# E and F stacked on 128 partitions and turned together, the last unit of the first chunk normalised by VectorE, A's turns placed anew

## Chip, cores and metric

One core of one Trainium2 chip. The metric is the device time of one execution in microseconds; the median of several executions is given. The kernel before takes 569.17 us (569.0 to 570.17 in 4 runs).

Below, "weights" without more are those of the feed-forward part. "Projection" is the product of E with K; the program's name for its result is `kvp`.

## The reference, cut to what matters

```python
k_proj = einsum('ks,bhsd->bhkd', E, k)           # E, F: 64 x 1024; k, v: 8 x 8 x 1024 x 64, f32
v_proj = einsum('ks,bhsd->bhkd', F, v)
attn   = softmax(q @ k_proj.T / 8)               # per head, 64 keys
x      = (attn @ v_proj) as 8192 x 512
out    = (silu(x @ w_gate) * (x @ w_val)) @ w_out   # 512 -> 1536 -> 512
```

## The kernel before

The work is a stream of 16 chunks of 512 tokens. Attention of later chunks is woven into the feed-forward matmuls of earlier ones, so TensorE hardly ever stands still. Only the first chunk has nothing to hide behind: its K, E, F, V, q and weights have to arrive, E and F have to be turned (their 1024 positions must lie on partitions), and then come the projection of K, the scores, the softmax in four "units", the turn of the attention matrix A, the product with V, and the first feed-forward matmuls. The change touches this start only.

```python
def warm(n):                       # n matmuls on zeros; keep TensorE's clock up
    ps = bank("v", [P, CW], FP32, "warm")
    for _ in range(n): nc.tensor.matmul(out=ps[:], lhsT=zeros[:, 0:P], rhs=zeros[:], ...)

def u_N(b, u, eng=nc.gpsimd):      # normalise one unit: ee * rr, 128 x 512
    ...
    eng.tensor_tensor(out=..., in0=ee..., in1=rr...to_broadcast([P, 4, 2, KP]), op=ALU.mult)

# transfers at the start
for i in range(2):
    nc.scalar.dma_start(out=kraw[i][:], in_=k[0, 2*i : 2*i+2]...)      # heads 0-1, 2-3
for which, src in (("E", E), ("F", F)):
    raw = const.tile([KP, S], FP32, name=f"{which}raw")                # 64 partitions each
    (nc.sync if which == "E" else nc.scalar).dma_start(out=raw[:], in_=src)
...
# order of work, cut and shortened (u_T turns q, u_KT0 turns the projected K, u_S scores and exp,
# u_A turns A, u_V0 projects V, u_PV1 and u_PV2 multiply A with V, f_mm feed-forward matmuls)
warm(11); turn(E); warm(4)
cast kraw -> kb (VectorE; half of head 3 by ScalarE)
u_KV(0, "k", (0, 4)); warm(1)      # first projection
u_T, u_KT0; turn(F, half 0); u_T; u_S(0, 0) ...; turn(F, half 1); warm(1)
u_KV(0, "k", (4, 8)) ...           # second projection, then scores, units 2, 1, 3
u_N(0, 3)                          # on GpSimd
u_V0(0, 2); u_PV2; warm(1); u_V0(2, 3); u_A(0, 2); u_V0(3, 4)
u_PV1(2); u_PV1(3); u_A(0, 1)
f_mm(gate of f=0); u_A(0, 3); u_PV2; f_mm(value of f=0) ...
```

The casting loads (K's heads 4 to 7, q, V, the weights) are issued by GpSimd on one queue; E, F and K's heads 0 to 3 come by the hardware queues of SyncE and ScalarE.

The softmax here doesn't subtract the row's maximum and nothing guards it: scores larger than these inputs give would overflow.

Of the kernel before, what the change touches and what calls it, by code (L numbers as in the profile page):

```python
# [12 lines left out]
BF16 = mybir.dt.bfloat16  # L13
FP32 = mybir.dt.float32
# [3 lines left out]
S = 1024  # L18
D = 64
KP = 64  # L20
DM = H * D
DFF = 1536
P = 128
NJ = S // P
# [10 lines left out]
def kernel(  # L35
# [19 lines left out]
    nc = tc.nc  # L55
    scale = 1.0 / float(D) ** 0.5

    const = ctx.enter_context(tc.tile_pool(name="const", bufs=1))
# [15 lines left out]
    BD = [const.tile([P, H, P], BF16, name=f"BD{i}") for i in range(2)]  # L74
    BDV = [const.tile([P, NPAIR, P], BF16, name=f"BDV{i}") for i in range(2)]
    ks = [const.tile([P, H, D], BF16, name=f"ks{i}") for i in range(2)]
    ET = const.tile([P, NJ, KP], BF16, name="ET")
    FT = const.tile([P, NJ, KP], BF16, name="FT")

    wg = w_pool.tile([P, NKT, DFF], BF16, name="wg")  # L80
    wv = w_pool.tile([P, NKT, DFF], BF16, name="wv")
# [51 lines left out]
    def bank(where, shape, dt, name):  # L133
        pool, tag = banks[where]
        return pool.tile(shape, dt, name=name, tag=tag)

    def copy(eng, out, in_):
        (nc.scalar.copy if eng is nc.scalar else eng.tensor_copy)(out=out, in_=in_)  # L138
# [152 lines left out]
    def u_N(b, u, eng=nc.gpsimd):  # L291
        ch, w = divmod(u, 4)
        g, i = divmod(w, 2)
        if (b, ch) in BY_DMA:
            if (b, ch, "d") not in AA:
                AA[b, ch, "d"] = aw.tile([P, 4, H, KP], BF16, name="AAd", tag="AAd")
            a = AA[b, ch, "d"][:, 2 * i : 2 * i + 2, 4 * g : 4 * g + 4, :]
        else:
            a = AA[b, u] = aw.tile([P, 2, 4, KP], BF16, name="AA", tag="AA", bufs=4)
            a = a[:]  # L300
        eng.tensor_tensor(  # L301
            out=a.rearrange("p j h k -> p h j k"),
            in0=ee.pop((b, u))[:],
            in1=rr.pop((b, u))[:].unsqueeze(3).to_broadcast([P, 4, 2, KP]),
            op=ALU.mult,
        )
# [45 lines left out]
    def u_PV1(b, ch, pr, i, eng):  # L352

        ps = ps_a.tile([P, CW // 2], FP32, name="pv", tag="pa")
        nc.tensor.matmul(
            out=ps[:].rearrange("p (j t) -> p j t", t=P),
            lhsT=BDV[b % 2][:, pr, :],
            rhs=AT[b, ch][:, 2 * i : 2 * i + 2, pr, :],
            start=True,
            stop=True,  # L360
        )
        copy(eng, xT[b, ch][:, pr, 256 * i : 256 * (i + 1)], ps[:])
# [4 lines left out]
    half = {}  # L367
# [110 lines left out]
    with tc.manual_schedule():  # L478

        kb[0] = kv_pool.tile([P, H, NJ, D], BF16, name="kb", tag="kb")  # L480
        kraw = [aw.tile([P, 2, NJ * D], FP32, name="kraw", tag=tag) for tag in ("qTd", "AAd")]
        for i in range(2):
            nc.scalar.dma_start(
                out=kraw[i][:],
                in_=k[0, 2 * i : 2 * i + 2].rearrange("h (p j) d -> p h (j d)", j=NJ),
            )
        ef = []
        for which, src in (("E", E), ("F", F)):
            raw = const.tile([KP, S], FP32, name=f"{which}raw")
            (nc.sync if which == "E" else nc.scalar).dma_start(out=raw[:], in_=src)  # L490
            ef.append(raw)
        load_q(0, 0, (0, 2))
        load_k(0, 4, 8)
        zeros = const.tile([P, CW], BF16, name="zeros")
        nc.vector.memset(zeros[:], 0.0)
        make_identity(nc, ident_fp[:])
        make_identity(nc, ident_bf[:])
        nc.vector.memset(ks[0][64:P], 0.0)

        def turn(which, at, halves=(0, 1)):  # L500
            for half in halves:
                ps = bank(at, [P, 4, KP], FP32, "efp")
                for i in range(4):
                    j = 4 * half + i
                    nc.tensor.transpose(  # L505
                        out=ps[:, i, :],
                        in_=ef[which][:, bass.ds(j, P, step=NJ)],
                        identity=ident_fp[:KP, :KP],
                    )
                js = slice(4 * half, 4 * half + 4)  # L510
                copy(nc.scalar, (ET, FT)[which][:, js, :], ps[:])

        def warm(n):

            ps = bank("v", [P, CW], FP32, "warm")
            for _ in range(n):
                nc.tensor.matmul(  # L517
                    out=ps[:], lhsT=zeros[:, 0:P], rhs=zeros[:],
                    start=True, stop=True,
                )  # L520


        dve, act = nc.vector, nc.scalar
        load_q(0, 0, (2, 4))
        load_v(0, (0, 4, 6, 8))
        load_w_gv(0, 1)
        load_w_gv(1, 2, (0,))
        warm(11)
        turn(0, "v")
        warm(4)  # L530
        for h in range(4):
            for n in range(2):
                eng = act if (h, n) == (3, 1) else dve
                ds = slice(256 * n, 256 * (n + 1)) if h == 3 else slice(0, 512)
                if n == 0 or h == 3:
                    copy(eng, kb[0][:, h].rearrange("p j d -> p (j d)")[:, ds], kraw[h // 2][:, h % 2, ds])
        nc.vector.memset(BD[0][:], 0.0)
        u_KV(0, "k", (0, 4), at="y")
        warm(1)
        u_T(0, 0, "a", act)  # L540
        u_KT0((0, 2), "vg", (dve, dve, dve, act))
        turn(1, "a", (0,))
        u_T(0, 2, "a", act)
        u_S(0, 0, "g")
        u_R(0, 0)
        u_N(0, 0)
        load_w_gv(1, 2, (1,))
        load_w_gv(2, 4, (0,))
        turn(1, "a", (1,))
        warm(1)  # L550
        u_KV(0, "k", (4, 8), at="y")
        warm(1)
        u_KT0((2, 4), "vg", (dve, dve, act, act))
        u_T(0, 1, "a", dve)
        u_T(0, 3, "a", dve)
        u_S(0, 2, "g")
        u_A(0, 0, dve)
        u_R(0, 2)
        u_N(0, 2)
        u_S(0, 1, "g")  # L560
        u_R(0, 1)
        u_N(0, 1)
        u_S(0, 3, "v")
        u_R(0, 3)
        u_N(0, 3)
        u_V0(0, 2, "y")
        u_PV2(0, 0, 0, 0, act)
        warm(1)
        u_V0(2, 3, "y")
        u_A(0, 2, act)  # L570
        u_V0(3, 4, "v")
        u_PV1(0, 0, 2, 0, dve)
        u_PV1(0, 0, 3, 0, act)
        u_A(0, 1, dve)
        load_w_gv(2, 4, (1,))
        f_mm(0, 0, 0, 0)
        u_A(0, 3, act)
        u_PV2(0, 0, 0, 1, dve)
        f_mm(0, 0, 1, 0)
        f_mm(0, 1, 0, 0)  # L580
        u_PV2(0, 0, 1, 1, act)
        f_mm(0, 1, 1, 0)
        nc.vector.memset(ks[1][64:P], 0.0)
        nc.vector.memset(BD[1][:], 0.0)
        nc.vector.memset(BDV[1][:], 0.0)
        load_w_gv(4, 6)
        load_q(0, 1, hs=(0, 4))
        load_w_gv(6, 8)
        load_q(0, 1, hs=(4, 8))
        load_w_gv(8, 10)  # L590
        load_w_gv(10, 12)
        load_q(1, 0)
        load_k(1)
        load_wo(0)
        load_wo(1)

        for i, u in enumerate(range(4, 8)):
            put(11 + i, u_T, 0, u)
            put(13 + i, u_S, 0, u)
            put(14 + i, u_R, 0, u)  # L600
            put(14 + i, u_N, 0, u)
            put((17, 18, 20, 21)[i], u_A, 0, u, nc.scalar)
        put(19, u_PV, 0, 1, 0)
        put(20, u_PV, 0, 1, 1)
        put(22, u_PV, 0, 1, 2)
        put(22, u_PV, 0, 1, 3, nc.vector)
        put(20, load_v, 1)
        put(20, load_q, 1, 1)
        for b in range(1, B):
            place(b)  # L610
        for b in range(2, B):
            s0 = 48 * (b - 1) - (20 if b == 3 else 24)
            at = (43, 43, 44, 45) if b == 2 else (s0, s0 + 2, s0 + 4, s0 + 6)
            put(at[0], load_k, b)
            put(at[1], load_v, b)
            put(at[2], load_q, b, 0)
            put(at[3], load_q, b, 1)

        for s in slots:
            slots[s].sort(key=lambda x: x[0] not in (load_k, load_v, load_q))  # L620


        ypart = defaultdict(list)
        for c in range(B * CH - 1):
            for n in range(NFT):
                f = n if c else 4 + (2 * n + 1) // 3
                ypart[(c + 1) * NFT + f].append((c, n))

        for t in range(NIT):
            c, f = divmod(t, NFT)  # L630
            i = 1 if t < 2 else None
            f_g(c, f, i)
            run_slot(2 * t)
            f_v(c, f, i)
            for a in ypart.pop(t, ()):
                f_y(*a)
            run_slot(2 * t + 1)
        for n in range(9):
            f_y(B * CH - 1, n)
        f_y_last(B * CH - 1, 3)  # L640
        assert not slots and not ypart
# [29 lines left out]
```

## Time and profile before

| what, in the trace of before | us |
|---|---|
| span | 567.5 |
| TensorE busy | 561.1 |
| first projection starts | 8.24 |
| second projection starts | 12.47 |
| first value matmuls start (`vps`, f = 0) | 21.21 |
| value matmuls of f = 6 start | 33.43 |

The four starts are the milestones of this document. A shift of the last one is a shift of the end, because from there on TensorE works without a wait.

### The profile page before, as it was taken

The page shows a single profiled execution, that of the slowest core. Times are in us where ns is not written, and L with a number is a line of the kernel's source. Part 1 is how long each engine was busy: PE and PEld are TensorE (multiplying, and loading weights), DVE is VectorE, ACT ScalarE, POOL GpSimd, SP SyncE. Part 2 cuts the span into 40 slices and gives each one's busy share as a digit, 9 for nine tenths or more (in the row PEclk, how much of TensorE's full clock was granted, in tenths as well). Part 3 has the DMA queues.
Part 4 walks back from the last instruction along what each step waited for, and adds up shares of the span by engine and source line. Part 5 has one row for each costly group of instructions (what it writes and reads, how often), then busy time and mean ns, then how long its engine had stood idle before and what let it go on. Part 6 is the DMA issues. An engine that isn't in the chain of part 4 may idle for free.

```text
span 567.5 us, 7942 instructions
## 1 busy us (share of the span) xinstructions
PE 561.1 (99%) x2970; PEld 266.5 (47%) x2970; DVE 338.9 (60%) x576; ACT 235.7 (42%) x416; POOL 111.0 (20%) x124
## 2 busy tenths in 40 slices
PE   8999999999999999999999999999999999999997
PEld 4654444444444444444444444444444444444444
DVE  3786664766476645766466655666547665545550
ACT  3564452444435443443434434354343543443322
POOL 6951250124012400123002230023100220000000
PEclk9999999999999999999999999999999999999999
DMA  9999999729913795029940499106990213101012
GB/s 207 184 199 190 168 146 199 138 57 185 194 49 74 116 198 114 38 57 166 182 80 37 76 185 203 38 19 112 192 180 19 61 39 69 38 37 38 19 38 93
DMA packets 111159, 62.91 MB, mean 111 GB/s; under 512 B 64272, under 2 KB 102416, under 8 KB 111120
## 3 DMA queue, kind: packets, MB, share of 16 engines
q0 software_dynamic: 42816, 29.36, 36.1%
q1 hardware_dynamic: 67392, 31.46, 26.6%
q10 hardware_dynamic: 912, 1.57, 1.0%
q8 instruction: 23, 0.38, 0.3%
q14 instruction: 16, 0.13, 0.1%
HBM read 60.29 MB, written 16.78 MB: 136 GB/s over the span
## 4 chain that ended last, share of the span: by engine, by line
PE 95%; DMA 2%; POOL 1%; DVE 1%; ACT 0%; issue 0%; POOLq 0%
PE yps L415 29%; PE vps L377 28%; PE gps L377 28%; PE kvp L150 3%; PE sc L271 2%; PE pv L328 2%; DMA wv<-in_moe_w_val_dram 2%; PE warm L517 1%; PE efp L505 0%; POOL AA L301 0%; POOL wv L118 0%; POOL wg L118 0%; DVE BD L138 0%; PE kTp L194 0%; PE qTp L237 0%
## 5 line engine op out<-in xcount | busy, mean ns | idle before, releaser
L396 DVE SCALAR_TENSOR_TENSOR s<-th,gps 128x512 f32<-128x512 f32 x192 | 130.4, 679 | 134.6 <-ACT th L389 134.1
L377 PE MATMUL vps<-xT,wv 128*128 128x512 bf16 (+1 forms) x776 | 197.5, 377 | 0.4 <-DMA wv<-in_moe_w_val_dram 0.3
L377 PE MATMUL gps<-xT,wg 128*128 128x512 bf16 (+1 forms) x776 | 197.7, 377 | 0.1
L415 PE MATMUL yps<-wo,hT 128*128 128x512 bf16 (+1 forms) x780 | 194.5, 376 | 0.0
L389 ACT ACTIVATE th<-gps 128x512 f32<-128x512 f32 x192 | 114.6, 597 | 159.0 <-PE gps L377 153.9
L401 DVE TENSOR_TENSOR hT<-s,vps 128x512 bf16<-128x512 f32 x192 | 132.0, 687 | 20.4 <-DVE s L396 0.5
L301 POOL TENSOR_TENSOR AAd<-ee,rr 128x512 bf16<-128x512 f32 x56 | 58.3, 1043 | 342.3 <-issue 184.8
L415 PEld LDWEIGHTS <-hT 128*128 128x128 bf16 x780 | 76.2, 98 | 89.9
L377 PEld LDWEIGHTS <-wv 128*128 128x128 bf16 x776 | 73.8, 98 | 84.2 <-issue 2.9
L377 PEld LDWEIGHTS <-wg 128*128 128x128 bf16 x776 | 74.0, 98 | 81.3 <-issue 1.2
L425 ACT ACTIVATE ysb<-yps 128x512 f32<-128x512 f32 (+1 forms) x65 | 38.4, 591 | 77.7 <-PE yps L415 77.7
L138 ACT CAST xT<-pv 128x512 bf16<-128x512 f32 (+1 forms) x62 | 35.9, 582 | 52.3 <-PE pv L328 50.3
L286 DVE TENSOR_REDUCE zz<-ee 128x8 f32<-128x512 f32 x64 | 43.5, 679 | 22.4 <-ACT ee L275 22.4
L275 ACT ACTIVATE ee<-sc 128x512 f32<-128x512 f32 x64 | 37.9, 595 | 19.7 <-PE sc L271 18.5
L271 PEld LDWEIGHTS <-qTd 128*128 128x128 bf16 x224 | 17.2, 98 | 13.2 <-DMA qTd<-qb 0.2
L328 PE MATMUL pv<-AT,BDV 128*128 128x512 bf16 x60 | 22.4, 379 | 0.1
L271 PE MATMUL sc<-BD,qTd 128*128 128x128 bf16 x224 | 21.6, 219 | 0.0
L288 DVE RECIPROCAL rr<-zz 128x8 f32<-128x8 f32 x64 | 13.0, 203 | 6.7 <-DVE zz L286 0.5
L108 POOL DMA_DIRECT2D qb<-in_q_dram x18 | 16.3, 908 | 1.4 <-POOLq L655 0.8
L150 PE MATMUL kvp<-kb,ET 128*64 128x512 bf16 (+1 forms) x72 | 15.5, 358 | 0.0
L162 DVE CAST BDV<-kvp 64x256 bf16<-64x256 f32 x7 | 3.0, 426 | 20.0 <-ACT ks L158 17.8
L150 PE MATMUL kvp<-vb,FT 128*64 128x512 bf16 x56 | 13.4, 382 | 0.0
(64 smaller groups left out, 137.7 us busy)
## 6 DMA issues: line engine op xcount, KB each, us to landing
out_dram<-ysb SPq DMA_DIRECT2D x63, 256.0 KB, 2.3
qb<-in_q_dram POOLq DMA_DIRECT2D x14, 512.0 KB, 18.0
kb<-in_k_dram POOLq DMA_DIRECT2D x7, 1024.0 KB, 11.0
vb<-in_v_dram POOLq DMA_DIRECT2D x7, 1024.0 KB, 14.4
wo<-in_moe_w_out_dram POOLq DMA_DIRECT2D x2, 768.0 KB, 21.8
wg<-in_moe_w_gate_dram POOLq DMA_DIRECT2D x5, 256.0 KB, 8.0
wv<-in_moe_w_val_dram POOLq DMA_DIRECT2D x5, 256.0 KB, 9.6
kraw<-in_k_dram ACTq DMA_DIRECT2D x2, 512.0 KB, 4.9
```

The lines of the kernel that those rows point to most:

```text
L138: (nc.scalar.copy if eng is nc.scalar else eng.tensor_copy)(out=out, in_=in_)
L150: nc.tensor.matmul(out=t[lo : lo + 64, h0:h1].rearrange("p h d -> p (h d)"), lhsT=w[:, j, :], rhs=src[b][:, h0:h1, j, :], start=(j == 0), ...
L271: nc.tensor.matmul(out=ps[:, n, :], lhsT=t[:, n, :], rhs=BD[b % 2][:, 4 * g + n, :], start=True, stop=True)
L275: nc.scalar.activation(out=e[:].rearrange("p h j k -> p (h j k)"), in_=ps[:].rearrange("p a k -> p (a k)"), func=AF.Exp, scale=scale,)
L286: nc.vector.reduce_sum(out=z[:], in_=e[:], axis=AX.X)
L301: eng.tensor_tensor(out=a.rearrange("p j h k -> p h j k"), in0=ee.pop((b, u))[:], in1=rr.pop((b, u))[:].unsqueeze(3).to_broadcast([P, 4, 2 ...
L377: nc.tensor.matmul(out=ps[:, ts], lhsT=(wg, wv)[w][:, kt, f * P : (f + 1) * P], rhs=x[:, kt, ts], start=(kt == 0), stop=(kt == NKT - 1),)
L389: nc.scalar.activation(out=th[:], in_=ps[:], func=AF.Tanh, scale=0.5)
L396: nc.vector.scalar_tensor_tensor(out=s1[:], in0=th[:], scalar=1.0, in1=g[:], op0=ALU.add, op1=ALU.mult)
L401: nc.vector.tensor_tensor(out=hT[c][:, f, :], in0=s1[:], in1=ps[:], op=ALU.mult)
L415: nc.tensor.matmul(out=yy[c][:, cs], lhsT=hT[c][:, f, i * P : (i + 1) * P], rhs=wo[:, f, cs], start=(f == 0), stop=(f == NFT - 1),)
L425: nc.scalar.activation(out=ysb[:, cs], in_=yy[c][:, cs], func=AF.Copy, scale=0.5)
```

## The change

It means to have E and F in one tile of 128 partitions, so that eight turns do the work of sixteen and no turn of F interrupts the middle; to give the third normalisation in a row to VectorE, so that GpSimd is free to issue weights; and to turn A before the first gate matmuls.

```diff
-    ET = const.tile([P, NJ, KP], BF16, name="ET")
-    FT = const.tile([P, NJ, KP], BF16, name="FT")
+    EF = const.tile([P, NJ, 2 * KP], BF16, name="EF")
+    ET, FT = EF[:, :, 0:KP], EF[:, :, KP : 2 * KP]
...
-        for which, src in (("E", E), ("F", F)):
-            raw = const.tile([KP, S], FP32, name=f"{which}raw")
-            (nc.sync if which == "E" else nc.scalar).dma_start(out=raw[:], in_=src)
+        efraw = const.tile([P, S], FP32, name="efraw")
+        for i, src in enumerate((E, F)):
+            nc.sync.dma_start(out=efraw[64 * i : 64 * i + 64], in_=src)
...
-        warm(11)
-        turn(0, "v")
-        warm(4)
+        warm(12)
+        turn_ef()          # 8 transposes of 128 x 128 f32, 2 copies of 128 x 512 by ScalarE
+        warm(2)
...  (head 3 cast by VectorE alone; the two turns of F and three warm matmuls around
...   the second projection's work go, warm(3) comes)
-        u_N(0, 3)
+        u_N(0, 3, dve)
...
-        warm(1)
         u_V0(2, 3, "y"); u_A(0, 2, act); u_V0(3, 4, "v"); u_PV1(0, 0, 2, 0, dve)
+        u_A(0, 1, dve)
         u_PV1(0, 0, 3, 0, act)
-        u_A(0, 1, dve)
+        u_A(0, 3, act)
         load_w_gv(2, 4, (1,))
         f_mm(0, 0, 0, 0)
-        u_A(0, 3, act)
```

More of the change, by code (lines that the diff above doesn't have):

```diff
@@ L486 @@
             )
-        ef = []
-        for which, src in (("E", E), ("F", F)):
-            raw = const.tile([KP, S], FP32, name=f"{which}raw")
-            (nc.sync if which == "E" else nc.scalar).dma_start(out=raw[:], in_=src)
-            ef.append(raw)
+        efraw = const.tile([P, S], FP32, name="efraw")
+        for i, src in enumerate((E, F)):
+            nc.sync.dma_start(out=efraw[64 * i : 64 * i + 64], in_=src)
         load_q(0, 0, (0, 2))
@@ L498, with turn_ef @@
         nc.vector.memset(ks[0][64:P], 0.0)
-        def turn(which, at, halves=(0, 1)):
-            for half in halves:
-                ps = bank(at, [P, 4, KP], FP32, "efp")
+        def turn_ef():
+            for half in range(2):
+                ps = bank("gv"[half], [P, 4, 2 * KP], FP32, "efp")
                 for i in range(4):
-                    j = 4 * half + i
                     nc.tensor.transpose(
                         out=ps[:, i, :],
-                        in_=ef[which][:, bass.ds(j, P, step=NJ)],
-                        identity=ident_fp[:KP, :KP],
-                    )
-                js = slice(4 * half, 4 * half + 4)
-                copy(nc.scalar, (ET, FT)[which][:, js, :], ps[:])
+                        in_=efraw[:, bass.ds(4 * half + i, P, step=NJ)],
+                        identity=ident_fp[:],
+                    )
+                nc.scalar.copy(out=EF[:, 4 * half : 4 * half + 4, :], in_=ps[:])
         def warm(n):
@@ L527 @@
         load_w_gv(1, 2, (0,))
-        warm(11)
-        turn(0, "v")
-        warm(4)
+        warm(12)
+        turn_ef()
+        warm(2)
         for h in range(4):
-            for n in range(2):
-                eng = act if (h, n) == (3, 1) else dve
-                ds = slice(256 * n, 256 * (n + 1)) if h == 3 else slice(0, 512)
-                if n == 0 or h == 3:
-                    copy(eng, kb[0][:, h].rearrange("p j d -> p (j d)")[:, ds], kraw[h // 2][:, h % 2, ds])
+            copy(dve, kb[0][:, h].rearrange("p j d -> p (j d)"), kraw[h // 2][:, h % 2])
         nc.vector.memset(BD[0][:], 0.0)
         u_KV(0, "k", (0, 4), at="y")
-        warm(1)
         u_T(0, 0, "a", act)
         u_KT0((0, 2), "vg", (dve, dve, dve, act))
-        turn(1, "a", (0,))
         u_T(0, 2, "a", act)
@@ L548 @@
         load_w_gv(2, 4, (0,))
-        turn(1, "a", (1,))
-        warm(1)
+        warm(3)
         u_KV(0, "k", (4, 8), at="y")
@@ L564 @@
         u_R(0, 3)
-        u_N(0, 3)
+        u_N(0, 3, dve)
         u_V0(0, 2, "y")
         u_PV2(0, 0, 0, 0, act)
-        warm(1)
         u_V0(2, 3, "y")
```

## The prediction

> **What bounds the kernel now.** I read the page first, then the waits of TensorE, then the timeline and the chain of waits of the first 40 us, then the landing times of the transfers that the change touches.
>
> ```profile
> PE 561.1 (99%) x2970; PEld 266.5 (47%) x2970; DVE 338.9 (60%) x576; ACT 235.7 (42%) x416; POOL 111.0 (20%) x124
> PEclk9999999999999999999999999999999999999999
> ...
> PE 95%; DMA 2%; POOL 1%; DVE 1%; ACT 0%; issue 0%; POOLq 0%
> ```
>
> TensorE (PE) is busy for 561.1 of 567.5 us at full clock. What is not useful matmul work lies in the start-up, before the steady stream at about 24 us. The diff touches nothing else: the order of instructions of the changed program differs from the old one only there. Only some 20 us of 569 can react, and much of that is fixed by transfers. The waits of TensorE in the first 60 us:
>
> ```profile
> PE warm L517 <- DVE zeros L495: 1.2, 1, 1.2
> PE pv L343 <- ACT BDV L185: 0.5, 1, 0.5
> PE vps L377 <- DMA wv<-in_moe_w_val_dram: 0.3, 1, 0.3
> PE pv L355 <- ACT AT L138: 0.2, 1, 0.2
> ```
>
> The third line is a wall: the first matmul of the value branch cannot start before its weights land. The timeline puts it here:
>
> ```profile
> 7.99 0.77 POOL L118 DMA_DIRECT2D wv<-in_moe_w_val_dram  x1
> ...
> 21.21 0.61 PE L377 MATMUL vps<-xT,wv 128*128 128x256 bf16 x4 [0.30 <-DMA wv<-in_moe_w_val_dram]
> ```
>
> Issued at 7.99 and 13.2 us under way (the longest landing in the view of that line), it lands at 21.17. The GpSimd queue moves about 200 GB/s from 8 us on without a hole, so this landing is set by the bytes queued ahead. A second wall is in the chain of waits:
>
> ```profile
> 19.02 1.03 POOL AA L301
> 20.05 0.76 POOL wv L118
> ...
> 23.74 9.64 DMA wv<-in_moe_w_val_dram
> ```
>
> These weights land at 33.38 and their first matmul starts at 33.43. The matmul group before it started at 32.93 and streams 0.22 us (the chain gives 0.22 for such groups of four), so TensorE stood about 0.28 us there: an estimate from these numbers. Time won before 21 us is kept only if both landings come earlier too. The part that is moved, E's and F's way to the first projection, is this:
>
> ```profile
> 0.74 0.58 SPq L490 DMA_DIRECT2D Eraw<-in_E_dram  x1
> 1.77 0.54 ACTq L490 DMA_DIRECT2D Fraw<-in_F_dram  x1
> 6.15 1.11 PE L505 MATMUL efp<-ident_fp,Eraw 64*128 64x64 f32 x8
> 7.27 0.86 DVE L138 CAST kb<-kraw 128x512 bf16<-128x512 f32 x2 [1.70 <-DMA kraw<-in_k_dram]
> 8.24 1.06 PE L150 MATMUL kvp<-kb,ET 128*64 128x256 bf16 x8
> ```
>
> E lands at 6.02 (5.3 us after issue), the second K transfer at 7.25 (6.0 us), F at 8.92 (7.2 us). The 11 warming matmuls end just when E arrives. Today the first projection at 8.24 waits for E and for K's casts but not for F: F is turned in two halves between later work, at 10.01 and 11.57.
>
> **What the Trainium skill says.** Page "DMA: Bandwidth & Descriptors", section "Queues, rings and completion order": each DMA engine takes turns between the queues at the granularity of a packet. The trace agrees: the packet records show the first K transfer at 1.88 to 3.9 us, E (64 packets of 4096 bytes on SyncE's queue) at 3.6 to 4.7, the second K transfer at 4.3 to 6.6, F at 6.7 to 7.7; on one engine after another E's first packet starts about 5 ns after K's last, and K's second 5 ns after E's. So the queues alternated, one whole transfer's share at a time. The same page, "Issuing engines are not separate DMA queues": moving an issue to another engine saves only issue time, since all run on the same 16 DMA engines. Page "TensorE: Matmul & The Clock Gate", section "The HAM clock gate": the clock drops only after an idle window of some 3.4 us. No such gap is in this trace, and a wait of 2 us should not cool it. Page "SBUF — State Buffer", section "SBUF: two separate sides": a VectorE operation with two SBUF inputs and a GpSimd operation that reads SBUF lock each other out. No row here shows that pair, so it is open.
>
> **The change part by part.**
>
> 1. E and F by one queue. F's issue moves from 1.77 (third on ScalarE) to about 1.32 (0.74 + 0.58, second on SyncE), a saving of 0.45 us at issue. If queues alternate as above, the order stays K, E, K, F. F then follows the second K transfer directly, without the 0.4 us hole that the packets show between the end of most of its packets (6.28) and F's first (6.69). I expect F to land at about 8.2 to 8.6 instead of 8.92.
>
> 2. Turning together. Eight transposes over 128 columns replace sixteen over 64. Eight of 64 take 1.11 us, with starts some 0.12 us apart (6.2 to 7.0 in the view of that tile). Twice the columns means about 0.23 us apart: 8 x 0.23 = 1.8 us, an estimate. The two F halves disappear from the middle (0.60 + 0.58 us in the chain), so 1.11 + 1.18 = 2.29 becomes 1.8: 0.5 us less TensorE work. ScalarE has two copies of 0.59 us (row of 128x512 f32 to bf16) for four of 0.37 to 0.39: 0.3 us less. But all 1.8 us now lies ahead of the first projection, and so does F's landing. This is the cost that I think decides.
>
> 3. Start of the projection. Landing 8.4 + 0.1 + 1.8 + two warm matmuls of 0.22 = 10.5 us, against 8.24: 2.2 us later. TensorE idles from the end of the 12 warm matmuls (1.19 + 12 x 0.43 = 6.4; a cold one takes 0.43) to 8.4.
>
> 4. What the middle gives back. From the start of the first projection to the start of the second is 4.23 us now (8.24 to 12.47). The way to the first scores is unchanged, because the BD copies set it (10.06 to 11.27). After the scores, at 11.64, F's half and one warm matmul go (0.58 + 0.32) and three warm matmuls come (0.65): 0.2 us back. The warm matmul between the small projections of V goes too: 0.2 us.
>
> 5. K's casts. Head 3 is no longer split with ScalarE; a whole head takes 0.477 us against 0.517 for the half beside ScalarE. No cost.
>
> 6. The last unit normalised by VectorE. On GpSimd one takes 1.04 us and the third runs from 19.02 to 20.05; on VectorE such a two-tensor operation takes 0.69 us (row of hT), in a hole of VectorE from 18.43 to 19.60. GpSimd issues the next weights 1.03 us earlier. But the queue is full at that time, so I count at most the 0.28 us at the second wall.
>
> 7. The A turns. Their four-matmul groups (0.22 us each) move ahead of the first gate matmuls. The work is the same and the order only helps if their inputs are ready: 0.
>
> Sum at the first wall: +2.2 - 0.2 - 0.2 = +1.8 us for the work arriving there. TensorE has 0.30 us of waiting to spend at 21.21, leaving +1.5. The second wall absorbs another 0.28: +1.2, or 570.4 us.
>
> **The rivals.** (a) F follows E directly on its queue, before the second K transfer. The 12 warm matmuls (end 6.4) look sized for such a landing near 6.6. K then lands about 0.8 us later, at 8.1, its two casts end at 9.1, and the projection starts at 9.1 (+0.9). Parts 4 and the 0.30 us of slack swallow nearly all of it, and part 6 gives up to 0.28: 569.0 us. For it speaks the sizing; against it the alternation of packets. (b) GpSimd's earlier issues bring the later weights down and a denser start of the hardware queues (the dip at 4.5 to 5.5 us, about 200 GB/s between stretches of 340) brings everything queued behind 0.3 to 0.5 us earlier. Both walls then move and TensorE keeps up: 568.5. Against it: the latency of 9.64 us at 23.74 is queueing, not issue. (c) The shared port holds VectorE's normalisation until GpSimd's runs out at 19.05. Then VectorE's xT copy, now 19.60, is 0.15 us later or so, which the wall hides under (a) and adds under the main path: 570.6. (d) TensorE cools while it waits for F; matmuls of 0.43 instead of 0.22 us for one window would add 1 us or more: 571.5.
>
> **Range and chances.** I weigh the main path with (c) and (d) at a little over half (570.4 and up) and (a) with (b) at a little under half (568.5 to 569.1). The middle is 569.8 us. The three runs of before already spread from 569.0 to 570.17, so a range of 568.5 to 571.2 should hold it 8 times in 10. Two per cent is 11.4 us, most of the start-up, which nothing here can move: within 2% at 0.98, faster 0.01, slower 0.01.
>
> **What would show it.** The landing of F (issue plus time under way): near 8.4 means the main path, near 6.6 rival (a). The start of the first kvp group: 10.5 or 9.1. The first transposes of efp: 8 in about 1.8 to 2 us. A TensorE wait before efp of about 2 us, or none. The vps group now at 21.21: at about 22.7 and without a DMA wait on the main path, still near 21.2 and with one under (a), below 20.9 under (b). GpSimd should show three AA groups in the first 24 us instead of four, and the weight issue now at 20.00 near 19.1 plus the delay of the work before. I am wrong if the second wall moves by a microsecond with GpSimd's issues, if the transposes are much longer than 0.23 us apart, or if something beyond 40 us changes at all.

## The result, and the profile after

The changed kernel takes 570.6 us (570.07 to 571.49 in 4 runs) against 569.17. The ratio is 1.0023, with a 95% interval of 1.0005 to 1.0041. (Ratios here are the mean time of one kernel's fast runs over that of the other's fast runs of the same rounds, so not quite the ratio of the medians.) The loss is clear of noise and far within 2%.

First the line of engine busy times and the clock, from the page of the changed kernel; they answer to the lines of before in the prediction:

```profile
PE 560.7 (99%) x2961; PEld 266.3 (47%) x2961; DVE 340.4 (60%) x577; ACT 235.1 (41%) x413; POOL 110.1 (19%) x123
PEclk8999999999999999999999999999999999999999
```

TensorE has 0.4 us less to do, and the span is 1.6 us longer (569.1). So the time went into waits, and the first digit of the clock row is an 8 where it was a 9. The waits of TensorE in the first 60 us of the changed kernel (total, times, longest):

```profile
PE efp L503 <- DMA efraw<-in_F_dram: 1.9, 1, 1.9
PE warm L514 <- DVE zeros L493: 1.2, 1, 1.2
PE pv L343 <- ACT BDV L185: 0.5, 1, 0.5
PE sc L271 <- DVE BD L138: 0.5, 1, 0.5
PE pv L355 <- ACT AT L138: 0.2, 1, 0.2
PE aTp L317 <- DVE xT L138: 0.2, 1, 0.2
```

A wait of 1.9 us for F has come in, and the wait for the value weights has gone. The timeline of the same stretch (start, duration, engine, line, operation):

```profile
1.19 5.30 PE L514 MATMUL warm<-zeros 128*128 128x512 bf16 x12 [1.19 <-DVE zeros L493]
1.38 0.57 SPq L489 DMA_DIRECT2D efraw<-in_F_dram  x1
8.41 1.12 PE L503 MATMUL efp<-ident_fp,efraw 128*128 128x128 f32 x8 [1.92 <-DMA efraw<-in_F_dram]
9.89 1.91 PE L150 MATMUL kvp<-kb,EF 128*64 128x256 bf16 x8
14.74 1.06 PE L150 MATMUL kvp<-kb,EF 128*64 128x256 bf16 x8
20.74 1.13 DVE L301 TENSOR_TENSOR AA<-ee,rr 128x512 bf16<-128x512 f32 x1
23.13 0.60 PE L377 MATMUL vps<-xT,wv 128*128 128x256 bf16 x4
35.06 1.03 PE L377 MATMUL vps<-xT,wv 128*128 128x512 bf16 x4
```

Read it by the milestones. The first projection starts 1.65 us later (9.89 against 8.24), the second 2.27 later, the value matmuls 1.92 later, those of f = 6 only 1.63 later, and the span grew by 1.6. Two things were not in my sum. The first projection lasted 1.91 us where the second, the same work, lasted 1.06. And VectorE's normalisation lasted 1.13 us where 0.69 was expected. The first is explained by the table of stretches of the changed kernel; the column after the busy times is the clock granted to TensorE, then come DMA share and GB/s:

```profile
8.00:10.00 2.00, 1.59 (x11) 1.19 (x12) 1.07 (x3) 0.87 (x2) 1.32 (x3) 0.96 1.39 204
10.00:12.00 2.00, 2.00 (x11) 1.38 (x12) 0.00 (x0) 0.36 (x2) 0.33 (x1) 0.50 1.52 190
12.00:14.00 2.00, 1.46 (x16) 0.99 (x14) 0.86 (x3) 1.25 (x4) 0.00 (x0) 0.68 1.39 204
14.00:16.00 2.00, 2.00 (x15) 1.09 (x12) 0.89 (x2) 1.06 (x3) 0.00 (x0) 1.00 1.23 204
```

0.96, 0.50 and 0.68 mean half clock from about 9.84 (0.16 us of 8 to 10) to about 13.28 us (1.28 us of 12 to 14): one stretch of 3.4 us. It does not happen in every execution. The mean clock of a whole execution tells: one such stretch costs 3.4 x 0.5 / 569 = 0.003 of it. The four executions of the changed kernel had 570.30 and 570.07 us at a clock of 1.0, and 570.89 and 571.49 at 0.997. I call these warm and cold below; warm means a mean clock of at least 0.999.

### The profile page after: what moved, and what is told of

Read it like the earlier page. It is cut to its first block, busy times and chain, and to the rows that moved or that the text cites. A ratio compares the mean times of both kernels' runs of the same rounds, so it can differ in the third digit from the quotient of the medians.

```text
span 569.1 us, 7918 instructions
## 1 busy us (share of the span) xinstructions
PE 560.7 (99%) x2961; PEld 266.3 (47%) x2961; DVE 340.4 (60%) x577; ACT 235.1 (41%) x413; POOL 110.1 (19%) x123
## 4 chain that ended last, share of the span: by engine, by line
PE 96%; DVE 1%; DMA 1%; ACT 0%; issue 0%; SPq 0%
PE gps L377 29%; PE yps L415 29%; PE vps L377 29%; PE kvp L150 3%; PE sc L271 2%; PE pv L328 2%; DMA efraw<-in_F_dram 1%; DVE zz L286 0%; DVE BD L138 0%; PE qTp L237 0%; ACT th L389 0%; DVE AA L301 0%; PE efp L503 0%; PE warm L514 0%; PE aTp L317 0%
## 5 line engine op out<-in xcount | busy, mean ns | idle before, releaser
L150 PE MATMUL kvp<-kb,EF 128*64 128x512 bf16 (+1 forms) x72 | 16.4, 374 | 0.0
L150 PE MATMUL kvp<-vb,EF 128*64 128x512 bf16 x56 | 13.4, 382 | 0.0
```

The lines of the kernel that those rows point to most:

```text
L150: nc.tensor.matmul(out=t[lo : lo + 64, h0:h1].rearrange("p h d -> p (h d)"), lhsT=w[:, j, :], rhs=src[b][:, h0:h1, j, :], start=(j == 0), ...
```

## The experiments

Theory 1: the first projection now waits for F, and this carries through to the end. Theory 2: the VectorE normalisation costs. Theory 3: the last part of the change helps and hides some of the loss. Rival A: the clock makes part of the loss. All outputs are right. Milestones are those of each kernel's one profiled execution.

### The parts alone

`x_ef_only` is the changed kernel with its last part (from `u_N(0, 3, dve)` to the second `u_A`) as before:

```diff
-        u_N(0, 3, dve)
+        u_N(0, 3)
...      (warm(1) back; u_A(0, 1) after u_PV1(3), u_A(0, 3) after the gate matmuls)
```

> The changed kernel with its last part undone: the last unit is normalised by GpSimd again, the A turns stand where they stood, the warm matmul between V's projections is back. Theory 1 (E and F together bring the loss, because the first projection now waits for F at 8.3 us): the loss against the kernel before stays, 1.0 to 1.5 us, so 570.2 to 570.7. Theory 2 (part of the loss is the VectorE normalisation, which took 1.13 us in the changed kernel where 0.69 was expected, and sits on the chain of waits ahead of the xT copy): this kernel is 0.3 to 0.5 us faster than the changed one, near 570.1, and its first value matmuls (23.13 in the changed kernel) start 0.2 to 0.5 us earlier if the clock is the same. Theory 3 (the last part helps, as meant): this kernel is slower than the changed one by 0.2 us or more.

Measured: 571.72 us (570.25 to 572.63), ratio 1.0044 (1.0031 to 1.0058). Four of the five executions were cold (571.39 to 572.63), the warm one took 570.25. So E and F bring the loss, as theory 1 has it; theory 2 expected this kernel to be faster than the changed one, with its value matmuls 0.2 to 0.5 us earlier, and it is not: they start at 23.23 against 23.13 (F landed at 8.40 against 8.27, and both profiles are cold). In the profile, TensorE waits 0.6 us at 37 us for q, which the changed kernel does not. This points to theory 3, but most of the difference is in cold executions, so a warm version had to follow.

`x_turns_only` is the kernel before with this last part alone.

```diff
-        u_N(0, 3)
+        u_N(0, 3, dve)
...      (warm(1) gone; u_A(0, 1) before u_PV1(3), u_A(0, 3) before the gate matmuls)
```

> The kernel before with the last part of the change alone: VectorE normalises the last unit, A turns as in the change, E and F as before. Theory 1: no loss without E and F, the first value matmuls still start at about 21.2 us behind their weights and the time is that of before within 0.3 us (568.9 to 569.5). Theory 2 (the VectorE normalisation costs by itself): VectorE's normalisation takes over 0.9 us here too because GpSimd's own normalisation ends at 19.05, and the time is 0.3 us or more over before. Theory 3 (the part helps): GpSimd issues its weights 1 us earlier, the second wall at 33.4 us moves, and the time is 0.3 us or more under before.

Measured: 569.12 us, the same median as the kernel before in these rounds, ratio 1.0003 (0.999 to 1.0017); four warm executions from 569.01 to 569.15 and one cold of 570.3. The normalisation took over 0.9 us, as theory 2 expected, but the time did not rise: the first wall hides it. Two lines of its timeline, the group that VectorE does and the value matmuls:

```profile
18.53 1.13 DVE L301 TENSOR_TENSOR AA<-ee,rr 128x512 bf16<-128x512 f32 x1
21.32 0.61 PE L377 MATMUL vps<-xT,wv 128*128 128x256 bf16 x4 [0.24 <-DMA wv<-in_moe_w_val_dram]
33.26 1.03 PE L377 MATMUL vps<-xT,wv 128*128 128x512 bf16 x4
```

From the first value matmuls to those of f = 6 it takes 33.26 - 21.32 = 11.94 us, against 33.43 - 21.21 = 12.22 before: 0.28 us less, which is the second wall of the prediction, to the digit. The weights of f = 6 landed at 31.42 instead of 33.38, since GpSimd issued them at 22.78 instead of 23.74 (and they landed just before an instruction fetch came, see the first wall below). So theory 3's mechanism works, and it is worth less than the 0.3 us that it expected of the time.

### The clock

`x_warm20` keeps TensorE busy for longer ahead of the turns.

```diff
-        warm(12)
+        warm(20)
         turn_ef()
```

> The changed kernel with 20 warm matmuls instead of 12 ahead of the turns, so that TensorE is busy while it waits for F (the wait of 1.9 us becomes about 0.2 us; F lands at 8.3 us as before). Theory A (the wait lets the clock drop for one window in some executions, as in the profiled one where the clock was 0.5 from 9.8 to 13.3 us): no stretch at half clock after 7 us in this profile, the first projection takes 1.06 us and not 1.91, and the time is 0.3 to 0.6 us under the changed kernel with a smaller spread: 570.0 to 570.3. Theory B (the clock has no part in it, the wait alone does): the same time as the changed kernel, 570.6.

Measured: 570.39 us (570.34 to 570.62), ratio 1.0022 (1.001 to 1.0035), all five executions at 0.999 or more. The same stretches of its trace:

```profile
8.00:10.00 2.00, 1.22 (x10) 1.09 (x10) 1.48 (x3) 0.50 (x2) 0.82 (x3) 1.00 1.49 200
10.00:12.00 2.00, 1.87 (x20) 1.23 (x19) 0.00 (x0) 1.21 (x4) 0.67 (x1) 1.00 1.42 194
```

The clock stays at 1.00, the projection takes 1.06 us, and the spread is 0.3 us; the time lies just over the 570.0 to 570.3 expected. F landed late in this profile (8.64, against 8.27 in the changed kernel's), and yet the value matmuls start at 22.60, before the changed kernel's 23.13. The cold stretch cost that profile 0.53 us there, and 0.37 more that the earlier F should have brought: 0.9 us, an estimate from these numbers. The wait for F fell only to 1.1 us, not to 0.2: warm matmuls at full clock are shorter than I had counted.

`x_after_again` is the changed kernel unedited, five more executions, and a profile.

> The changed kernel itself, five more executions, to see its two kinds. Theory A: executions at a mean clock of 0.999 or more take 570.0 to 570.4, those at 0.997 or less (one window or more of half clock) take 570.8 or more, and both kinds occur. If the clock has no part in it, time and mean clock do not go together.

Measured: 571.58 us (571.19 to 572.75), ratio 1.0040 (1.0027 to 1.0052), and all six executions cold (0.994 to 0.997). No warm one occurred, so the run does not compare the kinds within itself. The two sets of the changed kernel together hold two warm executions of ten: 570.07 and 570.30, against 570.89 to 572.75 for the cold ones. This fits rival A; the expected mixture in these rounds did not come. In the kernel before, four of the 38 executions with a listed clock of the later rounds were at 0.997 (570.06 to 570.35): it has this state too, but seldom. The clock does not explain every slow execution: one of these 38 took 570.7 at 1.0.

### When F lands: the dose

`x_f_third` exchanges the queues of F and of K's second half, `x_f_third_warm18` does the same with 18 warm matmuls, and `x_f_act_warm20` puts F third on ScalarE's queue as in the kernel before, with 20 warm matmuls.

```diff
 # x_f_third: order of issue            # x_f_act_warm20
-ScalarE: K0, K1   SyncE: E, F          -ScalarE: K0, K1     SyncE: E, F
+ScalarE: K0, F    SyncE: E, K1         +ScalarE: K0, K1, F  SyncE: E
```

> The changed kernel with the queues of F and of the second K transfer exchanged: K first half and F on ScalarE's queue, E and K second half on SyncE's. If the queues alternate, one whole transfer's share at a time, the order becomes K, E, F, K: F lands near 6.6 us instead of 8.3 and the second half of K near 8.3 instead of 7.5. The first projection then waits for K's casts, at 9.2 to 9.4 us instead of 9.9, and TensorE's wait before the turns is gone: 569.7 to 570.0. If the landing order is set otherwise (by the time of issue), F stays behind the second half of K and the time stays at 570.6.

Measured: 569.42 us (569.2 to 570.77), ratio 1.0007 (0.9995 to 1.002). The profiled execution was the cold one (570.77); the four warm ones took 569.2 to 569.48. In that profile F landed at 7.78, between the two expectations: F's packets and the second half of K's ran at the same time, some engines serving one first and some the other. The time fell by more than expected all the same.

> x_f_third (K, E, F, K) with 18 warm matmuls. If the one slow run of x_f_third (570.77 against 569.2 to 569.5) came from the clock: all five runs at a clock of 0.999 or more, 569.2 to 569.6. In the profile F lands at 7 to 7.8 us, the turns take 1.1 us and not 1.94, and the first projection starts at 9.5 to 10.0 behind K's casts, earlier than x_warm20's 10.27. If the joint turning costs whatever the order: 570.2 or more.

Measured: 569.51 us (569.41 to 570.15), ratio 1.0004 (0.9991 to 1.0016), all at 0.999 or more (the one of 570.15, at 1.0, lies over the 569.6 expected). Here F landed at 6.89, K's second half at 8.39, and the first projection started at 9.39, 0.1 us earlier than expected, behind VectorE's cast of K.

> x_warm20 with one edit: F's transfer third on ScalarE's queue again, as in the kernel before; E and F are still stacked and turned together. A dose test of theory 1. If the landing of F sets the first projection: F lands at 8.9 to 9.3 us instead of 8.6, the turns and the first projection (10.27 in x_warm20) start 0.3 to 0.7 us later, and the time rises by as much over x_warm20's: 570.7 to 571.1, ratio to before 1.0028 or more. If the sharing of engines between F's and K's queues is what costs, K's second half lands at 7.3 instead of 8.0 and the time falls to 570.0 or less.

Measured: 571.12 us (570.96 to 571.13), ratio 1.0027 (1.0014 to 1.004), all warm. (Three of the eleven executions of the kernel before in these rounds were cold, which makes this ratio small; 1.0028 or more was expected.) K's second half landed at 7.43, earlier than in `x_warm20` (7.98), and the time rose nevertheless. These are the first projections of `x_f_third_warm18`, `x_warm20` and `x_f_act_warm20`, from the three timelines:

```profile
9.39 1.03 PE L150 MATMUL kvp<-kb,EF 128*64 128x256 bf16 x8 [0.81 <-DVE kb L138]
```

```profile
10.27 1.06 PE L150 MATMUL kvp<-kb,EF 128*64 128x256 bf16 x8
```

```profile
11.01 1.06 PE L150 MATMUL kvp<-kb,EF 128*64 128x256 bf16 x8
```

| kernel, warm | F lands | first projection | value matmuls | median us |
|---|---|---|---|---|
| `x_f_third_warm18` | 6.89 | 9.39 | 21.70 | 569.51 |
| `x_warm20` | 8.64 | 10.27 | 22.60 | 570.39 |
| `x_f_act_warm20` | 9.38 | 11.01 | 23.34 | 571.12 |

From the first row to the second the last three columns rise by 0.88, 0.90 and 0.88; from the second to the third by 0.74, 0.74 and 0.73. Where F is what the projection waits for (the last two rows; in the first it is K's cast), F's delay passes to the end one to one in the traces. The medians come from three groups of runs, in which the kernel before took 569.28, 569.12 and 569.24 us; with these taken off, the losses are 0.23, 1.27 and 1.88 us, so the last step is 0.6 us rather than 0.73. In direction and rough size this is theory 1, shown; only one pair of rows tests the one to one.

### The queue by itself

`x_f_sp` is the kernel before with F on SyncE's queue behind E, and nothing else.

```diff
-            (nc.sync if which == "E" else nc.scalar).dma_start(out=raw[:], in_=src)
+            nc.sync.dma_start(out=raw[:], in_=src)
```

> The kernel before with one edit: F's transfer is issued on SyncE's queue right behind E instead of third on ScalarE's; E and F are still turned apart, F in two halves between later work. It tells the queue from the joint turning. Theory 1 (what costs is that the first projection waits for F; the queue itself is harmless): F lands at 8.2 to 8.7 us instead of 8.9 to 9.3, the first projection starts at 8.2 to 8.4, and the time is that of before within 0.3 us (568.9 to 569.4). If the queue itself costs (K's second half is delayed by F): the first projection starts at 8.8 us or later and the time is 569.6 or more.

Measured: 570.08 us (569.45 to 570.89), ratio 1.0011 (0.9999 to 1.0024); four warm executions of 569.45 to 570.19. The interval just holds 1, so a loss in time is likely but not shown. My expectation of a harmless queue was wrong all the same, by the profile. K's second half landed at 8.81 instead of 7.25, and TensorE waited for its cast:

```profile
9.51 1.03 PE L150 MATMUL kvp<-kb,ET 128*64 128x256 bf16 x8 [1.15 <-DVE kb L138]
```

On ScalarE's queue F stands behind K; on SyncE's it takes turns with K's second half. In the profiles with F there, K's second half landed at 7.48 to 8.81 (seven kernels); with F on ScalarE's behind K's halves, at 7.25, 7.39 and 7.43. In the changed kernel this costs nothing more, because its projection waits for F anyway: K's casts end at 8.6, the projection starts at 9.89.

### The last part, warm, and GpSimd against VectorE

`x_ef_warm20` is `x_ef_only` with `warm(20)`.

> The changed kernel with its last part undone (as x_ef_only) and with 20 warm matmuls, so that the clock stays up. Against x_warm20 (570.4) it shows what the last part does when the clock is up. If the last part is neutral: 570.2 to 570.6. If VectorE's normalisation costs: 570.1 or less. If the last part helps (GpSimd's earlier issues keep the weights and q ahead of TensorE): 570.7 or more, with a TensorE wait for a transfer between 33 and 40 us, as x_ef_only's 0.6 us for q.

Measured: 571.0 us (570.36 to 571.43), ratio 1.0029 (1.0015 to 1.0043), all at 0.999 or more. It is slower than `x_warm20` by 0.6 us, partly because F landed at 8.90 and not 8.64. Its value matmuls start at 22.76 (0.16 later, so the last part itself does not speed up the way there). In these profiles the last part even costs 0.1 us on that way. Then the kernel without it loses this, in its timeline:

```profile
34.46 0.39 PE L237 MATMUL qTp<-ident_bf,qb 128*128 128x128 bf16 x4
35.17 1.04 PE L377 MATMUL vps<-xT,wv 128*128 128x512 bf16 x4 [0.32 <-DMA wv<-in_moe_w_val_dram]
```

The group before streams 0.22 us, so TensorE could have gone on at 34.68 and stood 0.49 us: the second wall, which `x_warm20` passes without a wait (its weights of f = 6 land at 32.90, these at 35.12). Theory 3 holds: in the changed kernel the last part saves about half a microsecond at the second wall (one profile of each kernel).

`x_no_pool` gives VectorE the normalisations of units 2 and 1 as well.

```diff
-        u_N(0, 2)            # and u_N(0, 1)
+        u_N(0, 2, dve)       # and u_N(0, 1, dve)
```

> The changed kernel with units 2 and 1 of the first chunk normalised by VectorE as well, so that GpSimd computes nothing while VectorE normalises unit 3. If GpSimd's normalisation holds VectorE's back (shared way to SBUF): VectorE's three normalisations take 0.55 to 0.70 us each instead of 1.13. If 1.13 us is what this operation costs VectorE (f32 with a broadcast operand): 1.1 us each again. The time may be longer either way, as VectorE carries two more units.

Measured: one look, cold, 572.26 us. VectorE's three normalisations:

```profile
19.75 0.69 DVE L301 TENSOR_TENSOR AA<-ee,rr 128x512 bf16<-128x512 f32 x1
21.31 0.69 DVE L301 TENSOR_TENSOR AA<-ee,rr 128x512 bf16<-128x512 f32 x1
22.87 0.69 DVE L301 TENSOR_TENSOR AA<-ee,rr 128x512 bf16<-128x512 f32 x1
```

0.69 us each with GpSimd at rest, 1.13 us beside GpSimd's. In the changed kernel GpSimd's two run from 19.28 to 21.32, and VectorE's from 20.74 to 21.87, so 0.55 us of it lie behind GpSimd's end. That GpSimd's operation holds VectorE's back, rival (c), is shown.

### Tries at a better kernel

`x_ef_first` issues E and F first, one per hardware queue, so that they are turned while K is under way (the order of issue in words).

```diff
+        SyncE: E, K0    ScalarE: F, K1
-        warm(12); turn_ef(); warm(2)
+        warm(9); turn_ef(); warm(9)
-            copy(dve, kb... head h)
+            copy(act if h == 3 else dve, kb... head h)
-        warm(3)
+        warm(1)
```

> A try at a better kernel from what the runs showed: E and F are issued first, one on each hardware queue, K's halves behind them, so that the joint turns run while K is still under way; head 3 is cast by ScalarE beside VectorE's head 2; 9 + 9 warm matmuls around the turns; one instead of three before the second projection. F lands near 4.6 to 5 us, K's second half near 8.3, the first projection starts at 8.8 to 9.0. If the first wall (value weights at about 21.2 us when an instruction fetch falls into their way, else 20) and the second are then what is left: 568.9 to 569.3, a tie with the kernel before. Better than 568.8 would need both walls to be missed; over 569.5 would mean that TensorE's start-up chain is longer than I think.

Measured: 569.41 us (569.22 to 569.7), all warm, ratio 0.9999 (0.9987 to 1.0011): a tie, as expected, though just over the range of 568.9 to 569.3. F landed at 5.85 and K's second half at 8.56, both later than expected, and the first projection started at 9.26 and not at 8.8 to 9.0. The second started at 12.74, and TensorE reached the value matmuls in time to wait for them:

```profile
21.94 0.61 PE L377 MATMUL vps<-xT,wv 128*128 128x256 bf16 x4 [0.55 <-DMA wv<-in_moe_w_val_dram]
```

`x_fewer` takes 11 warm matmuls out of it (`warm(7)`, `warm(2)`, none around the second projection).

> x_ef_first with 11 warm matmuls fewer (7 and 2 around the turns, none before and after the second projection), so that TensorE reaches any given piece of work some 22 instructions earlier in its stream. If the 16 KB fetches that delay the value weights are TensorE's own instructions, fetched as it gets through its stream, the fetch of 19.86 us comes 0.3 to 0.5 us later and misses the value weights: they land 0.7 to 0.8 us behind the gate weights (near 20.3) and not 2.4 behind (21.90), TensorE's wait of 0.55 us for them is gone, and the time is 568.6 to 569.0, under the kernel before. If the fetch is not tied to the instruction count, it stays at 19.8 to 19.9, the weights land near 21.9 and the time stays at 569.2 to 569.7. If the clock drops in the gap of 1.7 us that the missing warm matmuls leave, the mean clock is 0.997 and the time 570 or more.

Measured: 570.0 us (569.51 to 571.34), ratio 1.0008 (0.9994 to 1.0022). Its profile fell on the coldest execution (clock 0.991, three stretches of 3.4 us in a row), so it does not decide what it was made for: the fetch came at 22.17 us, but TensorE was late as well (its value weights landed 0.74 us behind the gate weights, as for a fetch that misses them). The three warm executions took 569.51 to 570.0, so the expected gain did not come.

No kernel here is faster than the kernel before by more than noise; `x_turns_only` and `x_ef_first` tie with it, and the intervals of `x_f_third`, `x_f_third_warm18`, `x_f_sp` and `x_fewer` hold 1 too.

### Why the first wall stands where it stands

The prediction took the landing of the value weights at 21.17 us for a matter of bytes queued ahead. In the changed kernel, with the same bytes ahead, they landed at 19.73. The difference lies with one packet. The queues that moved data from 19 to 20.2 us, before:

```profile
q0 software_dynamic: 821, 0.20, 173.4%
q8 instruction: 1, 0.02, 4.9%
```

A single packet of 16 KB of instructions took one of the 16 DMA engines for 0.945 us (its packet record).

| kernel | gate weights land | instruction fetch starts | value weights land | behind gate weights |
|---|---|---|---|---|
| before | 19.14 | 19.14 | 21.17 | 2.03 |
| `x_turns_only` | 19.30 | 19.25 | 21.28 | 1.98 |
| `x_ef_first` | 19.54 | 19.86 | 21.90 | 2.36 |
| `x_f_act_warm20` | 19.22 | 19.81 | 19.96 | 0.74 |
| `x_warm20` | 19.31 | 20.17 | 20.06 | 0.75 |
| changed | 18.99 | 20.41 | 19.73 | 0.74 |

Where the fetch starts by 0.3 us after the gate weights, the value weights are late; from 0.6 us on they are not. The other eight traces fit: their fetches start 0.8 us or more after the gate weights, and the value weights land 0.73 to 0.75 us behind these. Similarly the weights of f = 6 landed late (33.38, 35.12) in before and in `x_ef_warm20`, with fetches at 31.31 and 33.06. Whose instructions are they? At the second fetch TensorE (matmuls and weight loads) had started 454 to 464 instructions in all 14 traces, although its time varied from 31.3 to 36.2 us; so it goes with TensorE's own progress. The first fetch is looser, 215 to 308. That the fetch delays the weights is read off these traces; no run moved the fetch alone. The delay over the usual 0.74 us is 1.24 to 1.62 us, longer than the fetch's 0.945, and what makes up the rest is open.

## Why the prediction was right

The time lies in the range (570.6 in 568.5 to 571.2), 0.8 us above the stated middle and 0.2 above the main path of 570.4. Luck had a part in it: two of the four executions were warm, and in the later rounds, with all six cold, the same kernel had a median of 571.58, outside the range. By its steps:

1. **Order of the transfers: right.** The packets came K, E, K, F, and F landed at 8.25 to 8.40 in the four profiles with 12 warm matmuls, and at 8.64 and 8.90 in the two with 20, where 8.2 to 8.6 was expected. Rival (a), F near 6.6, fell. The 12 warm matmuls were no evidence for an early landing. What the step did not have is that F and K's second half slow each other on two queues (`x_f_sp`).

2. **Cost of the joint turns: wrong in size.** "Twice the columns means about 0.23 us apart" failed. Eight turns of 128 columns took 1.12 us, as long as eight of 64 had taken (1.11), so TensorE's turning fell from 2.29 to 1.12 us, not to 1.8. The weight loads ahead of the turns keep the weight-load row busy 0.96 us in both traces, so it is likely they that set the pace, and the moving columns hide behind them; I did not test this alone.

3. **Start of the projection: close, but by errors that cancelled.** The terms written there sum to 10.7 and not to 10.5 (two warm matmuls are 0.44, and one was added). The warm kernel `x_warm20` measured 8.64 + 0.14 + 1.13 + 0.36 = 10.27. The changed kernel started at 9.89 with F at 8.27. The missing 0.7 us of turns about made up for the slip and for the late landing.

4. **What the middle gives back: right.** In `x_warm20` the lag behind the kernel before shrinks from +2.03 us at the first projection (10.27 against 8.24) to +1.74 at the second (14.21 against 12.47) and +1.39 at the value matmuls. Expected were +2.2, +2.0 and +1.5.

5. **K's casts without the split: no cost**, as said; they ended before EF was there.

6. **The normalisation by VectorE: wrong in duration, right in effect.** "In a hole of VectorE ... 0.69 us" failed: 1.13 us, because GpSimd's normalisation held it, rival (c). It stands on the chain ahead of the xT copy, where TensorE waits 0.2 us (`aTp` for `xT`). GpSimd's earlier issues then saved the 0.28 us at the second wall that were counted, and 0.49 us where the start was later (`x_ef_warm20`). The prediction's own sign of being wrong, that the second wall moves by a microsecond with GpSimd's issues, came for the landing (31.42 for 33.38 in `x_turns_only`, 1.96 us, with an instruction fetch out of the way); of the time it was worth only the 0.28.

7. **A's turns: 0**, not separable from part 6 in these runs.

**The two walls.** The second was sized right (0.28 us, `x_turns_only`). The first was sized right and explained wrong, as far as the traces tell: not only bytes but an instruction fetch in the way of one DMA engine.

**The clock: wrong.** "A wait of 2 us should not cool it" failed. It stood there as rival (d), at 571.5; it came in eight of ten executions of the changed kernel. It cost about 0.9 us in the profiled one, and it is why the median is 570.6 and, in the later rounds, 571.58. The warm loss alone is 1.27 us (570.39 against 569.12) by `x_warm20`, and 0.9 to 1.1 us by the changed kernel's own two warm executions. So the main path's 1.2 us is about what warm executions lose; what lies above is the clock.

Why did `x_f_act_warm20` stay warm, though TensorE stood 1.9 us before its turns too? The clock records of the traces point to the answer. In each of the six traces with a cold stretch the clock fell 3.41 us after it had risen to full, and TensorE had stood for 1.91 to 2.54 us of these 3.41. In the changed kernel the clock rose at 6.44 us and fell at 9.85, with the wait from 6.49 to 8.41 wholly between. In `x_f_act_warm20` it rose at 5.10, so such a stretch ends at 8.51, in the middle of the wait from 7.59 to 9.52: TensorE stood for 0.92 us of one stretch and 1.01 us of the next. Counted in this way, in steps of 3.41 us from the rise to 40 us, TensorE stood for at most 1.51 us of any step in the eight traces that stayed warm. So in these 14 traces the idle time within one step tells them apart, and the length of the wait does not. The rise itself came between 3.99 and 7.19 us, which may be why one kernel has warm and cold executions; no warm execution of the changed kernel was profiled to show it. What lets the clock rise again stays open: `x_fewer` stayed at half for three steps with 1.57, 0.49 and 0.46 us of idle time, `x_f_third` for one with 0.52. In all four kernels with 18 or 20 warm matmuls no execution of 20 was cold.

## What to carry to other kernels

Joining two small jobs makes the first user wait for the later of the two inputs: before merging, look up when each lands and who waits for it, not how many instructions are saved. Work at the start that is off the chain is free; put on the chain it passes to the end one to one, here 0.74 us for 0.74. When the time of one kernel splits into two groups, look at the mean clock of each execution before explaining the difference.

## What the Trainium skill lacked or had wrong

- "TensorE: Matmul & The Clock Gate", section "The HAM clock gate", has the clock drop after an idle window of some 3.4 us. Here it dropped, for one stretch of 3.4 us, after a wait of 1.9 us (changed kernel, half clock from 9.84 to 13.28 us), in eight of ten executions. The length of the stretch agrees with the window it gives. The page has no rule for partly idle windows. Here 1.91 us or more of idle time in a step of 3.41 us went with a drop (six traces), and 1.51 us or less did not (eight).
- "SBUF — State Buffer", section "SBUF: two separate sides", says that a VectorE operation with two SBUF inputs and a GpSimd operation that reads SBUF lock each other out. It holds here: 1.13 us beside GpSimd, 0.69 us without (`x_no_pool`). The prediction cited it and left it open; it should have been counted.
- "DMA: Bandwidth & Descriptors", section "Queues, rings and completion order": taking turns between queues was enough to foresee the order K, E, K, F, but no page gives a size for how much one transfer then delays the other. Here K's second half landed at 7.25 to 7.43 with F behind it on its own queue, and at 7.48 to 8.81 with F on the other.
- "Runtime: NRT & Kernel Launch", section "Terms", says that instruction memory is refilled in blocks of 16 KiB. The traces show packets of 16384 bytes. The same page's section "Instruction fetch mechanics" counts 256 instructions to a block; that fits the 250 or so TensorE matmuls and weight loads between fetches here (about 460 at the second, about 710 at the third). It calls the cost mostly hidden. That such a refill takes a DMA engine for 0.945 us and goes with weights that land 1.3 us late, for which TensorE waited 0.30 us in the kernel before, no page that I read has.
- No page that I read gives the pace of f32 turns: eight took 1.11 us with 64 moving columns and 1.12 with 128.
